# GpSimd is left out of the Fourier stage, its rows lie in four tiles, and the first weights are converted beside the folds

## The chip, the cores and the metric

One core of a Trainium2 chip runs the whole program. The metric is the device time of one execution in microseconds (us); the kernel before takes 2784.65 us, median of three runs from 2784.36 to 2785.43 us. TensorE multiplies matrices, VectorE and ScalarE and GpSimd work on elements, SyncE issues most of the transfers. In the profile they are PE (and PEld for its weight loads), DVE, ACT, POOL and SP.

## What is computed

The reference, cut to what matters:

```python
X = np.fft.fft(np.fft.fft(x, axis=1), axis=2).real         # x: 4 x 3072 x 256
h = X.reshape(-1, 256) @ w_in                              # 256 x 2048
g = np.where(h > 0, h, np.exp(np.minimum(h, 0)) - 1)
y = (g @ w_out).reshape(4, 3072, 256)                      # 2048 x 256
h2 = np.maximum(y @ w_in2, 0)                              # 256 x 1024
u, v = h2[..., :512], h2[..., 512:]
v = (v - mean(v)) / sqrt(var(v) + 1e-6)                    # over the last axis
v = einsum("ts,bsd->btd", w_spatial, v) + b_spatial        # 3072 x 3072
out = (u * v) @ w_out2                                     # 512 x 256
```

The weights arrive as 64-bit numbers, as pairs of 32-bit words, and are converted on the chip.

## The kernel before

The program has four parts on one core: the Fourier transform along the sequence, the first weights (merged with the transform along the 256), the two-layer network, and the product with the 3072 x 3072 matrix. Products are done in three matmuls of a high and a low part (lines 181 to 183), so every operand needs a high part, rounded by ScalarE, and a low part, the rest, by another engine (`split`, lines 145 to 148).

The Fourier stage runs over four batches `b` and three blocks `i` of 128 rows: twelve blocks. For a block the rows and their mirror images (1032 KB, `load_q`) are folded in place into sums and differences (`fold`, seven instructions, lines 253 to 262); four slices of the result are split (`lhs`); TensorE then multiplies them with tables of cosines and sines in eight groups, 36 matmuls (`group`). The sums of a batch are added up in PSUM over its three blocks and copied out by ScalarE in the next batch's first block (`evac`, line 325), two pairs ahead of that block's `lhs` and two behind. In the first batch the tables are split too, a third per block (`split_table`). A single row, number 384, is folded by itself (`rows384`), and three pieces of it are put into row 0 (`row0`).

The order on every engine is the order in which the program is written. Queues run each by themselves and wait only for semaphores, so a transfer on SyncE's queue starts when all the ones ahead of it have been issued and its own buffer is free. In the kernel before a batch's rows lie in one tile of three blocks, two such tiles in turn. GpSimd does the rows 384, most of the tables' low parts, and in the batches after the first parts of the folds of blocks 1 and 2 (lines 253 and 255).

The first weights, 256 x 2048, are converted in eight pieces `q`. `from_f64` (lines 150 to 167) does a piece: two passes of ScalarE (156, 157), VectorE's lines 158, 159, 160 and 165, a multiplication on GpSimd (166) and an addition (167), which is handed back to be done later. VectorE's line 160 is the last that reads the piece as loaded. Pieces 0 to 5 are converted behind the last block, while TensorE does that and the sums of the middle rows (`sum_rows`, tiles `pm`). Pieces 6 and 7 come in the part behind, where the first weights are multiplied with the second transform (tiles `pw`); in the same loop the conversion of twelve pieces of the next weights begins (`late_load`, `late_convert`, `late_split`), two in this loop and one in each of the first ten steps of the network. In these steps the low part of the network's activations (line 607) is shared between VectorE and GpSimd.

Of the kernel before, what the change touches and what calls it, by code (L numbers as in the profile page):

```python
# [123 lines left out]
def fourier_ffn_gated_kernel(ctx: ExitStack, tc: tile.TileContext, t, out: bass.AP):  # L124
# [61 lines left out]
    with ExitStack() as ph:  # L186
# [4 lines left out]
        xop = pool("xop", bufs=4)  # L191
        qp = pool("qp", bufs=2)
        rp = pool("rp", bufs=2)
# [4 lines left out]
        to = [[tp.tile([P, 2, 2 * ODD], F32R, name=f"to{x}{i}") for x in "hl"] for i in range(3)]  # L198
        alt_raw = qp.tile([1, EVE], F32, tag="q", name="alt_raw")
        alt = tp.tile([1, EVE], F32R, name="alt")  # L200
# [7 lines left out]

        def load_q(b, sl):
            if b not in qs:  # L210
                qs[b] = qp.tile([P, 3, 4, 4, ND], F32, tag="q", name=f"q{b}")
            nc.sync.dma_start(qs[b][:, sl], t["xq"][b, :, sl])

# [16 lines left out]
        def split_table(i):  # L230
            v, g = nc.vector, nc.gpsimd
            for k, dst, eng in (("te", te, g if i else v), ("to", to, v if i == 2 else g)):
                for z, raw in enumerate(raw_tables.pop((k, i))):
                    split(dst[i][0][:, z], dst[i][1][:, z], raw, eng)
# [11 lines left out]
        def fold(b, sl, first=None):  # L246


            q, v = qs[b], nc.vector
            w = q[:, sl].rearrange("p i s k d -> p (i s) (k d)")  # L250
            u0, u1, cc, ss = (w[:, :, z * ND : (z + 1) * ND] for z in range(4))
            first = first or v
# [6 lines left out]
            g = q[:, sl].rearrange("p i s k d -> p i (s k) d")  # L259
            near, far = g[:, :, 0:6:5], g[:, :, 8:14:5]  # L260
            v.tensor_tensor(g[:, :, 2:8:5], near, far, op=ALU.add)
            v.tensor_tensor(g[:, :, 10:16:5], near, far, op=ALU.subtract)

        def halves_of(b, sl=slice(0, 3)):
            return qs[b][:, sl].rearrange("p i (h s) k d -> p (i h) (s k d)", h=2)

        def row0(b):

            q, r = halves_of(b), rs[b]
# [4 lines left out]
        def lhs(b, sl):  # L274

            q = halves_of(b, sl)
            ih = slice(2 * sl.start, 2 * sl.stop)
            for k, dst, c0, s0 in (("e", les, 2 * ND, 7 * ND + 1), ("o", los, 4 * ND, ND + 1)):
                if b not in dst:
                    dst[b] = [lp.tile([P, 6, 2, P], F32R, tag=f"l{x}", name=f"l{k}{x}{b}") for x in "hl"]  # L280
                for z, w0 in enumerate((c0, s0)):
                    split(*(x[:, ih, z] for x in dst[b]), q[:, :, w0 : w0 + P])

        def lhs_rest(b):
            q, r = halves_of(b), rs[b]
            for z, slot in ((0, 2), (1, 4)):
                nc.scalar.copy(raw_mids[:, z, :, b : b + 1], q[:, :, slot * ND + P : slot * ND + ND])
# [39 lines left out]

        everything = slice(0, 3)
        load_rows384(0)
        rows384(0)  # L330
        nc.scalar.dma_start(alt_raw, t["alt"])
        for i in range(3):
            load_q(0, slice(i, i + 1))
            if i < 2:
                load_table(i)
            if i == 0:
                load_rows384(1)
        nc.scalar.copy(alt, alt_raw)
        for b in range(B):
            if b:  # L340
                for i in range(3):
                    load_q(b, slice(i, i + 1))
                if b > 1:
                    load_rows384(b)
                rows384(b)
            for i in range(3):
                sl = slice(i, i + 1)
                fold(b, sl, nc.gpsimd if b and i else None)
                if b == 0:
# [6 lines left out]
                if i == 0:  # L356
                    row0(b)
                lhs(b, sl)
# [9 lines left out]
        def in_q(name, dtype):  # L368
            return qp.tile([P, 3, 4, 4, ND], dtype, tag="q", name=name).rearrange("p i s k d -> p (i s k d)")

        st = in_q("conv", U32)
        bits = [st[:, 1024 * x : 1024 * x + 1024].rearrange("p (n w) -> p n w", w=2) for x in range(3)]
        temps = [[st[:, n : n + 512] for n in range(3072 + 1536 * x, 4608 + 1536 * x, 512)] for x in range(2)]

        for q in range(3):
            load_w1(q, bits[q])
        raw_dt = rp.tile([P, 2, 2 * P + 2], F32, tag="r384", name="raw_dt")
# [3 lines left out]
        mid384 = [mp.tile([1, B], F32R, name=f"mid384{x}") for x in "hl"]  # L381
        mid_rows = in_q("mid_rows", F32)[:B, : 4 * EVE].rearrange("b (c n) -> b c n", c=4)
        st3 = lp.tile([P, 1536], U32, tag="lh", name="conv3")
        temps.append([st3[:, n : n + 512] for n in range(0, 1536, 512)])
        row_sums = {}
# [6 lines left out]

        left = None
        for q in range(6):
            mag, num, rest = temps[q % 3]
            left = convert_w1(q, bits[q % 3], mag, num, rest.bitcast(F32), between=left)
            if q + 3 < 6:
                load_w1(q + 3, bits[q % 3])
            if q == 1:
                split(*mids, raw_mids)  # L400
                split(*mid384, raw_mid384)
                evac(B - 1, 0)
            if q == 2:
                split(*dt, raw_dt)
                evac(B - 1, 1)
                for c in range(4):
                    sum_rows(c)
            if q == 3:
                evac(B - 1, 2)
                evac(B - 1, 3)  # L410
        left()
        for c in range(4):
# [75 lines left out]
    with tc.tile_pool(name="w1p", bufs=1, reuse_waits="tile", side="right") as w1p:  # L488
        w1_bits = [wr.tile([P, 512, 2], U32, tag="bits", bufs=2, name=f"w1b{q}") for q in (6, 7)]
        for q in (6, 7):  # L490
            load_w1(q, w1_bits[q - 6])
        QW = 512
# [12 lines left out]
        for q in range(DFF1 // QW):  # L505
# [17 lines left out]
            late_split()  # L523
            if q < 2:
                mag, num, rest = f64_temps(wr, 512)
                convert_w1(6 + q, w1_bits[q], mag, num, rest)()
                late_load(q)
            else:
                late_convert(q - 2)
            for z in range(2):  # L530
# [227 lines left out]
    for s in range(NG + LAG):  # L758
# [10 lines left out]
        late_split()  # L769
        late_convert(s + 2)  # L770
        if step == 0:
# [418 lines left out]
```

## Time and profile before

| | |
|---|---|
| median of three runs | 2784.65 us |
| the profiled execution, by itself | 2789.48 us |
| its span, first to last instruction | 2787.7 us |
| PE busy / DVE / ACT / POOL in the span | 2679.0 / 2107.6 / 1311.1 / 711.2 us |
| last matmul of the Fourier stage's middle rows (`pm`) starts | 138.59 us |
| the steps of the network that convert weights | 177 to 277 us |

A busy share is an average over the whole span. The Fourier stage is only its first twentieth, so what bounds it is read from that stretch alone. A row of a timeline has the start, the duration, the engine, the line, the operation, what is written and read, and in brackets how long the engine was idle before and what ended that. An instruction's duration holds its start-up, so two that follow each other overlap a little.

### The profile page before, as it was taken

What the parts mean: (1) busy time and instruction counts of PE and PEld (TensorE: products, weight loads), DVE (VectorE), ACT (ScalarE), POOL (GpSimd) and SP (SyncE); (2) the same over time, 40 slices, a digit from 0 to 9 for tenths busy, and PEclk for the clock granted to TensorE, in tenths of its full rate; (3) what the DMA queues carried; (4) which work ended last, traced back from release to release, by engine and by line L of the source; (5) the groups of instructions that cost most, each with busy time, mean ns of one, the idle gap of its engine ahead of it and who ended that gap; (6) DMA issues with size and microseconds to landing.
All of it is one profiled execution on the core that took longest, in us unless ns stands there. A gap on an engine that the chain in (4) does not pass through costs nothing.

```text
span 2787.7 us, 35149 instructions
## 1 busy us (share of the span) xinstructions
PE 2679.0 (96%) x12854; PEld 2363.4 (85%) x12854; DVE 2107.6 (76%) x2541; ACT 1311.1 (47%) x1676; POOL 711.2 (26%) x1079
## 2 busy tenths in 40 slices
PE   5867999999999999998999999999999999999999
PEld 5757999999999999997778888888888888888877
DVE  8878888888888888885667767676966577676775
ACT  3456767767767677774322332323233223322332
POOL 5267344455562444555130010000000000000000
PEclk8989999999999999999999999999999999999999
DMA  5531456667675566668799687677866777677683
GB/s 228 171 85 42 145 145 145 152 140 151 138 129 178 138 152 144 145 136 199 248 293 323 235 282 258 238 281 251 293 220 214 269 248 259 232 265 276 224 297 108
DMA packets 212592, 562.72 MB, mean 202 GB/s; under 512 B 24873, under 2 KB 49466, under 8 KB 210882
## 3 DMA queue, kind: packets, MB, share of 16 engines
q1 hardware_dynamic: 146584, 436.68, 44.8%
q0 software_dynamic: 43520, 92.29, 18.2%
q10 hardware_dynamic: 22314, 31.51, 3.1%
q8 instruction: 100, 1.64, 0.2%
q14 instruction: 74, 0.61, 0.1%
HBM read 396.77 MB, written 171.48 MB: 204 GB/s over the span
## 4 chain that ended last, share of the span: by engine, by line
PE 79%; DVE 9%; ACT 5%; DMA 3%; POOL 3%; issue 1%; ACTq 0%; SPq 0%; DVEq 0%; POOLq 0%
PE a L182 17%; PE a L183 16%; PE a L181 16%; PE acc L182 5%; PE acc L183 5%; PE acc L181 5%; DVE glo L607 2%; PE pv L183 1%; DMA u<-uu 1%; PE pv L181 1%; PE pv L182 1%; PE pe L181 1%; ACT ghi L600 1%; PE po L181 1%; PE po L182 1%
## 5 line engine op out<-in xcount | busy, mean ns | idle before, releaser
L182 PE MATMUL a<-wlo,vhi 128*128 128x512 f32 x1920 | 749.4, 390 | 4.5 <-DVE wlo L876 4.5
L183 PE MATMUL a<-whi,vlo 128*128 128x512 f32 x1920 | 749.3, 390 | 1.0 <-DVE vlo L876 1.0
L181 PE MATMUL a<-whi,vhi 128*128 128x512 f32 x1920 | 748.8, 390 | 1.0 <-ACT whi L870 1.0
L870 ACT CAST whi<-raw 128x1024 fp32r<-128x1024 f32 x240 | 252.7, 1053 | 812.6 <-PE a L183 437.0
L876 DVE TENSOR_TENSOR wlo<-raw,whi 128x1024 fp32r<-128x1024 f32 x240 | 293.6, 1223 | 370.2 <-ACT whi L870 369.9
L182 PEld LDWEIGHTS a<-wlo,vhi 128*128 128x128 f32 x1920 | 361.3, 188 | 81.5 <-DVE wlo L876 6.0
L181 PEld LDWEIGHTS a<-whi,vhi 128*128 128x128 f32 x1920 | 361.3, 188 | 77.1 <-ACT whi L870 1.4
L183 PEld LDWEIGHTS a<-whi,vlo 128*128 128x128 f32 x1920 | 361.4, 188 | 76.8 <-DVE vlo L876 1.5
L182 PE MATMUL acc<-glo,wo1h 128*128 128x384 f32 (+1 forms) x1024 | 352.2, 344 | 21.4 <-POOL glo L607 14.8
L183 PE MATMUL acc<-ghi,wo1l 128*128 128x384 f32 (+1 forms) x1024 | 349.6, 341 | 0.0
L181 PE MATMUL acc<-ghi,wo1h 128*128 128x384 f32 (+1 forms) x1024 | 349.5, 341 | 0.0
L607 DVE TENSOR_TENSOR glo<-h,ghi 128x1536 fp32r<-128x1536 f32 (+3 forms) x128 | 231.2, 1806 | 139.3 <-ACT ghi L600 139.3
L915 POOL DMA_DIRECT2D u<-u x32 | 24.4, 763 | 1173.0 <-DVE sum L932 723.2
L860 DVE TENSOR_TENSOR raw<-raw 128x1024 f32<-128x1024 f32 x240 | 293.0, 1221 | 11.0 <-DMA raw<-in_wT 7.8
L593 DVE SCALAR_TENSOR_TENSOR h<-e,h 128x1536 f32<-128x1536 f32 (+1 forms) x128 | 231.9, 1811 | 0.0
L582 ACT ACTIVATE e<-h 128x1536 f32<-128x1536 f32 (+1 forms) x128 | 190.0, 1485 | 88.8 <-DVE h L574 82.2
L182 PEld LDWEIGHTS acc<-glo,wo1h 128*128 128x128 f32 x1024 | 195.8, 191 | 28.4 <-POOL glo L607 17.3
L739 POOL DMA_DIRECT2D v<-v x226 | 204.7, 1259 | 52.9 <-DVE v L693 38.4
L600 ACT CAST ghi<-h 128x1536 fp32r<-128x1536 f32 (+1 forms) x128 | 187.8, 1468 | 24.5 <-DVE h L593 23.9
L183 PEld LDWEIGHTS acc<-ghi,wo1l 128*128 128x128 f32 x1024 | 196.1, 192 | 0.0
L181 PEld LDWEIGHTS acc<-ghi,wo1h 128*128 128x128 f32 x1024 | 195.3, 191 | 0.1
L587 ACT ACTIVATE e<-e 128x1536 f32<-128x1536 f32 (+1 forms) x128 | 190.2, 1486 | 0.0
(202 smaller groups left out, 4463.7 us busy)
## 6 DMA issues: line engine op xcount, KB each, us to landing
raw<-in_wT SPq DMA_DIRECT2D x480, 512.0 KB, 5.5
vlo<-v SPq DMA_DIRECT2D x120, 512.0 KB, 6.0
v<-v POOLq DMA_DIRECT2D x226, 256.0 KB, 5.9
v<-v SPq DMA_DIRECT2D x224, 256.0 KB, 3.0
u<-uu ACTq DMA_DIRECT2D x128, 192.0 KB, 3.3
u<-u POOLq DMA_DIRECT2D x16, 1024.0 KB, 9.4
q<-in_xq SPq DMA_DIRECT2D x12, 1032.0 KB
out<-sum SPq DMA_DIRECT2D x48, 256.0 KB, 2.3
```

The lines of the kernel that those rows point to most:

```text
L181: nc.tensor.matmul(acc, lhsT=w[0], rhs=x[0], start=start, stop=False, skip_group_check=more)
L182: nc.tensor.matmul(acc, lhsT=w[0], rhs=x[1], start=False, stop=False, skip_group_check=more)
L183: nc.tensor.matmul(acc, lhsT=w[1], rhs=x[0], start=False, stop=stop, skip_group_check=more)
L582: nc.scalar.activation(e[:, :, :w], st[s]["h"][:, :, :w], AF.Relu, scale=-1.0)
L587: nc.scalar.activation(e[:, :, :w], e[:, :, :w], AF.Exp, scale=-1.0)
L593: nc.vector.scalar_tensor_tensor(out=h[:, :, :w], in0=e[:, :, :w], scalar=-1.0, in1=h[:, :, :w], op0=ALU.add, op1=ALU.max)
L600: nc.scalar.copy(st[s]["hi"][:, :, :w], st[s]["h"][:, :, :w])
L607: eng.tensor_tensor(st[s]["lo"][:, z, :w], st[s]["h"][:, z, :w], st[s]["hi"][:, z, :w].bitcast(F32), op=ALU.subtract)
L739: nc.gpsimd.dma_start(dst, v, accum_op=ALU.add)
L860: nc.vector.tensor_tensor(res, total, y, op=ALU.add if sg > 0 else ALU.subtract)
L870: nc.scalar.copy(hi, total)
L876: nc.vector.tensor_tensor(lo, total, hi.bitcast(F32), op=ALU.subtract)
```

## The change

Four things are changed. A block's rows get a tile of their own, four in turn (`qp`, `load_q`), and the load of a block's rows is written at the head of that block. What GpSimd did in the Fourier stage goes to VectorE: the row 384, the tables' low parts, its part of the folds; only the multiplication of line 166 stays on GpSimd. The eight pieces of the first weights are converted beside the folds, one per block from the sixth block (batch 1, block 2) on and the eighth behind the last block; each conversion is followed by the load of the piece after the next. Pieces of the next weights take the places of pieces 6 and 7, so that the conversion ends two steps earlier in the network.

```diff
-        qp = pool("qp", bufs=2)
+        qp = pool("qp", bufs=4)
+        cvp = pool("cvp", bufs=1)
...
-        def load_q(b, sl):
-            if b not in qs:
-                qs[b] = qp.tile([P, 3, 4, 4, ND], F32, tag="q", name=f"q{b}")
-            nc.sync.dma_start(qs[b][:, sl], t["xq"][b, :, sl])
+        def load_q(b, i):
+            q = qs[b, i] = qp.tile([P, 4, 4, ND], F32, tag="q", name=f"q{b}{i}")
+            nc.sync.dma_start(q, t["xq"][b, :, i])
...
-            v, g = nc.vector, nc.gpsimd
-            for k, dst, eng in (("te", te, g if i else v), ("to", to, v if i == 2 else g)):
+            for k, dst in (("te", te), ("to", to)):
...
-            r, g = rs[b], nc.gpsimd
+            r, g = rs[b], nc.vector
...
-            first.tensor_tensor(w[:, :, : 2 * ND], w[:, :, : 2 * ND], w[:, :, 2 * ND :], op=ALU.add)
+            v.tensor_tensor(w[:, :, : 2 * ND], w[:, :, : 2 * ND], w[:, :, 2 * ND :], op=ALU.add)
             v.tensor_tensor(cc, u0, u1, op=ALU.add)
-            (v if b < 2 else first).tensor_tensor(ss, u0, u1, op=ALU.subtract)
+            v.tensor_tensor(ss, u0, u1, op=ALU.subtract)
...
+        def load_bits(q):
+            if q < 8:
+                raw = bits_at[q] = cvp.tile([P, 512, 2], U32, tag="bits", bufs=2, name=f"w1b{q}")
+                load_w1(q, raw)
+
+        def convert(q):
+            if left:
+                left.pop()()
+            if q < 8:
+                left.append(convert_w1(q, bits_at.pop(q), *f64_temps(cvp, 512)))
+                load_bits(q + 2)
...
         for b in range(B):
-            if b:
-                for i in range(3):
-                    load_q(b, slice(i, i + 1))
-                if b > 1:
-                    load_rows384(b)
-                rows384(b)
             for i in range(3):
-                sl = slice(i, i + 1)
-                fold(b, sl, nc.gpsimd if b and i else None)
+                if b:
+                    load_q(b, i)
+                if b == 1 and i == 1:
+                    load_bits(0)
+                    load_bits(1)
+                if b and i == 0:
+                    if b > 1:
+                        load_rows384(b)
+                    rows384(b)
+                fold(b, i)
...
                 if i == 2:
                     lhs_rest(b)
+                if b > 1 or b == 1 and i == 2:
+                    convert(step)
+                    step += 1
                 for c in range(4):
                     for z in range(2):
                         group(b, c, z, [i])
...
-        parts = [(nc.vector, slice(0, 2))] if s > len(late) - 2 else [(nc.vector, slice(0, 1)), (nc.gpsimd, slice(1, 2))]
+        parts = [(nc.vector, slice(0, 2))] if s > len(late) - 4 else [(nc.vector, slice(0, 1)), (nc.gpsimd, slice(1, 2))]
...
-        late_convert(s + 2)
+        late_convert(s + 4)
```

On SyncE's queue of the kernel before, from the last rows of batch 1 to the weights (`q1` to `q3` are the batches' tiles, `r384` the row 384, `conv` the tile of weights pieces):

```order
L212 DMA q1_493<-in_xq 128x2064 [waits DMAHW2_49]
L212 DMA q2_695<-in_xq 128x2064 [waits DMAHW3_49,DMAHW5_49,DVE_49,Activation_49]
L212 DMA q2_695<-in_xq 128x2064 [waits DMAHW7_49]
L212 DMA q2_695<-in_xq 128x2064 [waits DMAHW1_49]
L207 DMA r384_2_699<-in_x384 1x1032 [waits DMAHW2_49,DVE_49]
L212 DMA q3_899<-in_xq 128x2064 [waits DMAHW0_49,DVE_49,DMAHW3_49,Activation_49,Pool_49]
L212 DMA q3_899<-in_xq 128x2064 [waits DMAHW5_49]
L212 DMA q3_899<-in_xq 128x2064 [waits DMAHW7_49]
L207 DMA r384_3_903<-in_x384 1x1032 [waits DMAHW1_49,DVE_49]
L170 DMA conv_1103<-in_moe_w_in 128x1024 [waits DVE_49,DMAHW3_49,Activation_49,Pool_49]
```

Three loads of rows stand together, the weights behind all of them. The same queue now, from the last rows of batch 1 on (`q12` is batch 1, block 2; `w1b2` the weights piece 2):

```order
L212 DMA q12_652<-in_xq 128x2064 [waits DMAHW4_49,DVE_49,Activation_49]
L170 DMA w1b2_686<-in_moe_w_in 128x1024 [waits DMAHW2_49,DVE_49,Activation_49]
L212 DMA q20_726<-in_xq 128x2064 [waits DMAHW3_49]
L208 DMA r384_2_728<-in_x384 1x1032 [waits DMAHW5_49]
L170 DMA w1b3_786<-in_moe_w_in 128x1024 [waits DMAHW0_49,DVE_49,Activation_49]
L212 DMA q21_832<-in_xq 128x2064 [waits DMAHW1_49]
L170 DMA w1b4_862<-in_moe_w_in 128x1024 [waits DMAHW2_49,DVE_49,Activation_49]
L212 DMA q22_900<-in_xq 128x2064 [waits DMAHW3_49]
```

From batch 2 on a load of weights, which waits for VectorE and ScalarE, stands ahead of each load of rows. VectorE's queue now, from the low parts of batch 2, block 1, to the fold of block 2 (lines 251 to 260 are the fold's, `cv` the conversion's tiles):

```order
L148 TENSOR_TENSOR lol2_760<-q21_832,loh2_759 128x2x128 [waits Activation_49] x2
L167 TENSOR_TENSOR raw_w1l_219<-cv2_778,cv1_777 128x512 [waits Pool_49]
L158 TENSOR_SCALAR cv0_852<-cv0_852 128x512 [waits Activation_49]
L159 TENSOR_SCALAR cv1_853<-cv0_852 128x512 [waits DVE_49]
L160 SCALAR_TENSOR_TENSOR cv1_853<-w1b2_686,cv1_853 128x512 [waits DMAHW2_49,DVE_49]
L165 TENSOR_SCALAR cv0_852<-cv1_853 128x512 [waits DVE_49]
L251 TENSOR_TENSOR q22_900<-q22_900 128x4x258 [waits DMAHW3_49]
L252 TENSOR_TENSOR q22_900<-q22_900 128x4x129 [waits DVE_49]
L253 TENSOR_TENSOR q22_900<-q22_900 128x4x129
```

The five instructions of a conversion now stand between the low parts of a block and the next fold, and the fold's first instruction is back on VectorE.

## Rows read from the trace of the kernel before

**Rows 1.** Stretches: start:end length, busy us (instructions) of PE, PEld, DVE, ACT, POOL.

```profile
0.00:47.50 47.50, 20.43 (x76) 18.36 (x76) 40.64 (x38) 16.18 (x33) 30.05 (x24) 0.86 0.58 233
...
277.00:287.00 10.00, 10.00 (x59) 10.00 (x58) 8.65 (x14) 7.63 (x7) 5.00 (x8) 1.00 0.41 150
```

**Rows 2.** Waits to 128.8 us: total us, times, longest.

```profile
ACT leh L147 <- DVE q L262: 52.8, 8, 12.5
...
PE pa L181 <- ACT leh L147: 33.8, 5, 14.7
```

**Rows 3.** Timeline of VectorE: start, us, line, written<-read [idle before].

```profile
14.10 1.82 DVE L148 TENSOR_TENSOR tel<-raw_te,teh 128x770 fp32r<-128x770 f32 x2
...
47.63 1.22 DVE L253 TENSOR_TENSOR q<-q 128x1032 f32<-128x1032 f32 x1
48.88 0.69 DVE L254 TENSOR_TENSOR q<-q 128x516 f32<-128x516 f32 x1
...
51.90 0.42 DVE L262 TENSOR_TENSOR q<-q 128x258 f32<-128x258 f32 x1
53.97 0.76 DVE L148 TENSOR_TENSOR lel<-q,leh 128x256 fp32r<-128x256 f32 x2 [1.65 <-issue]
54.65 0.75 DVE L148 TENSOR_TENSOR lol<-q,loh 128x256 fp32r<-128x256 f32 x2
...
62.39 3.90 DVE L254 TENSOR_TENSOR q<-q 128x516 f32<-128x516 f32 x1
...
111.39 0.76 DVE L148 TENSOR_TENSOR lel<-q,leh 128x256 fp32r<-128x256 f32 x2 [0.47 <-ACT leh L147]
```

**Rows 4.** Timeline of VectorE, conversion of pieces 0 and 1 of the weights.

```profile
118.10 0.43 DVE L158 TENSOR_SCALAR conv<-conv 128x512 f32<-128x512 f32 x1 [0.28 <-ACT conv L156]
...
119.03 0.69 DVE L160 SCALAR_TENSOR_TENSOR conv<-conv 128x512 uint32<-128x512 uint32 x1
119.75 0.43 DVE L165 TENSOR_SCALAR conv<-conv 128x512 uint32<-128x512 uint32 x1
...
120.55 1.40 DVE L159 TENSOR_SCALAR conv<-conv 128x512 uint32<-128x512 uint32 x1
...
122.59 0.68 DVE L167 TENSOR_TENSOR raw_w1h<-conv 128x512 f32<-128x512 f32 x1
```

**Rows 5.** Timeline of GpSimd: a fold's first sum, and the conversion's multiplication.

```profile
63.72 2.01 POOL L253 TENSOR_TENSOR q<-q 128x1032 f32<-128x1032 f32 x1
...
120.32 1.34 POOL L166 TENSOR_TENSOR conv<-conv 128x512 f32<-128x512 f32 x1 [22.32 <-DVE conv L165]
```

**Rows 6.** Timeline: issue of the first rows, and VectorE's first instruction.

```profile
1.14 0.36 SPq L212 DMA_DIRECT2D q<-in_xq  x1
...
6.08 1.48 DVE L253 TENSOR_TENSOR q<-q 128x1032 f32<-128x1032 f32 x1 [6.08 <-DMA q<-in_xq]
```

**Rows 7.** Transfers to 185 us: queue, times, KB each, median us to landing.

```profile
a<-xo ACTq DMA_DIRECT2D x12, 384.0 KB, 7.8
conv<-in_moe_w_in SPq DMA_DIRECT2D x6, 512.0 KB, 4.2
```

**Rows 8.** Timeline of ScalarE: last store of an evacuation; a conversion's first pass.

```profile
57.03 0.52 ACTq L326 DMA_DIRECT2D a<-xo  x1
...
117.41 0.66 ACT L156 ACTIVATE conv<-conv 128x512 f32<-128x512 f32 x1
```

**Rows 9.** Stretches at two clocks (the last three: PE's clock, DMA share, GB/s).

```profile
102.00:106.00 4.00, 4.00 (x14) 4.00 (x13) 3.01 (x6) 1.81 (x5) 0.00 (x0) 0.50 1.01 361
107.00:111.00 4.00, 4.00 (x24) 4.00 (x24) 3.78 (x9) 2.32 (x7) 0.00 (x0) 1.00 0.83 313
```

**Rows 10.** Timeline of TensorE: first and last of 56 matmuls of the middle rows.

```profile
128.83 0.34 PE L181 MATMUL pm<-teh,midsh 128*4 128x386 f32 x1
...
138.59 0.34 PE L183 MATMUL pm<-toh,midsl 128*4 128x384 f32 x1
```

**Rows 11.** Timeline of VectorE: the same instruction in two steps of the network.

```profile
259.58 0.55 DVE L573 TENSOR_TENSOR h<-q,po 128x384 f32<-128x384 f32 x1 [1.18 <-POOL glo L607]
...
269.44 0.55 DVE L573 TENSOR_TENSOR h<-q,po 128x384 f32<-128x384 f32 x1 [1.18 <-POOL glo L607]
```

More of the change, by code (lines that the diff above doesn't have):

```diff
@@ L198, in fourier_ffn_gated_kernel @@
         to = [[tp.tile([P, 2, 2 * ODD], F32R, name=f"to{x}{i}") for x in "hl"] for i in range(3)]
-        alt_raw = qp.tile([1, EVE], F32, tag="q", name="alt_raw")
+        alt_raw = cvp.tile([1, EVE], F32, tag="cv0", name="alt_raw")
         alt = tp.tile([1, EVE], F32R, name="alt")
@@ L244, in rows384, with fold @@
             g.tensor_tensor(rv[:, 1, : 2 * ND], rv[:, 0, 2 * ND :], rv[:, 1, 2 * ND :], op=ALU.subtract)
-        def fold(b, sl, first=None):
-            q, v = qs[b], nc.vector
-            w = q[:, sl].rearrange("p i s k d -> p (i s) (k d)")
+        def fold(b, i):
+            q, v = qs[b, i], nc.vector
+            w = q.rearrange("p s k d -> p s (k d)")
             u0, u1, cc, ss = (w[:, :, z * ND : (z + 1) * ND] for z in range(4))
-            first = first or v
-            first.tensor_tensor(w[:, :, : 2 * ND], w[:, :, : 2 * ND], w[:, :, 2 * ND :], op=ALU.add)
+            v.tensor_tensor(w[:, :, : 2 * ND], w[:, :, : 2 * ND], w[:, :, 2 * ND :], op=ALU.add)
             v.tensor_tensor(cc, u0, u1, op=ALU.add)
-            (v if b < 2 else first).tensor_tensor(ss, u0, u1, op=ALU.subtract)
+            v.tensor_tensor(ss, u0, u1, op=ALU.subtract)
             x, y = w[:, 0::2], w[:, 1::2]
@@ L258, in fold, with halves_of @@
             v.tensor_tensor(y[:, :, : 2 * ND], x[:, :, 2 * ND :], y[:, :, 2 * ND :], op=ALU.subtract)
[L259 to L265, printed above, removed]
+            g = q.rearrange("p s k d -> p (s k) d")
+            near, far = g[:, 0:6:5], g[:, 8:14:5]
+            v.tensor_tensor(g[:, 2:8:5], near, far, op=ALU.add)
+            v.tensor_tensor(g[:, 10:16:5], near, far, op=ALU.subtract)
+        def halves_of(b, i):
+            return qs[b, i].rearrange("p (h s) k d -> p h (s k d)", h=2)
         def row0(b):
-            q, r = halves_of(b), rs[b]
+            q, r = halves_of(b, 0), rs[b]
             nc.scalar.copy(q[0:1, 0, 7 * ND : 8 * ND], r[:, 1, 1])
@@ L272, in row0, with lhs @@
             nc.scalar.copy(q[0:1, 1, 4 * ND : 5 * ND], r[:, 1, 0])
-        def lhs(b, sl):
-            q = halves_of(b, sl)
-            ih = slice(2 * sl.start, 2 * sl.stop)
+        def lhs(b, i):
+            q = halves_of(b, i)
+            ih = slice(2 * i, 2 * i + 2)
             for k, dst, c0, s0 in (("e", les, 2 * ND, 7 * ND + 1), ("o", los, 4 * ND, ND + 1)):
@@ L282, in lhs @@
                     split(*(x[:, ih, z] for x in dst[b]), q[:, :, w0 : w0 + P])
+            for z, slot in ((0, 2), (1, 4)):
+                nc.scalar.copy(raw_mids[:, z, ih, b : b + 1], q[:, :, slot * ND + P : slot * ND + ND])
         def lhs_rest(b):
-            q, r = halves_of(b), rs[b]
-            for z, slot in ((0, 2), (1, 4)):
-                nc.scalar.copy(raw_mids[:, z, :, b : b + 1], q[:, :, slot * ND + P : slot * ND + ND])
+            r = rs[b]
             nc.scalar.copy(raw_mid384[:, b : b + 1], r[:, 0, 0, P:])
@@ L326, in evac @@
             nc.scalar.dma_start(a_d[b][c], xo[:, :, :n])
-        everything = slice(0, 3)
+        bits_at, left = {}, []
+        def load_bits(q):
[8 more added lines that the diff above has]
+                load_bits(q + 2)
         load_rows384(0)
@@ L332, in fourier_ffn_gated_kernel @@
         for i in range(3):
-            load_q(0, slice(i, i + 1))
+            load_q(0, i)
             if i < 2:
@@ L338, in fourier_ffn_gated_kernel @@
         nc.scalar.copy(alt, alt_raw)
+        step = 0
         for b in range(B):
-            if b:
-                for i in range(3):
-                    load_q(b, slice(i, i + 1))
-                if b > 1:
-                    load_rows384(b)
-                rows384(b)
-            for i in range(3):
-                sl = slice(i, i + 1)
-                fold(b, sl, nc.gpsimd if b and i else None)
+            for i in range(3):
+                if b:
[8 more added lines that the diff above has]
+                fold(b, i)
                 if b == 0:
@@ L357, in fourier_ffn_gated_kernel @@
                     row0(b)
-                lhs(b, sl)
+                lhs(b, i)
                 if b and i == 0:
@@ L366, in fourier_ffn_gated_kernel @@
                         group(b, c, z, [i])
[L368 to L376, printed above, removed]
         raw_dt = rp.tile([P, 2, 2 * P + 2], F32, tag="r384", name="raw_dt")
@@ L381, in fourier_ffn_gated_kernel @@
         mid384 = [mp.tile([1, B], F32R, name=f"mid384{x}") for x in "hl"]
-        mid_rows = in_q("mid_rows", F32)[:B, : 4 * EVE].rearrange("b (c n) -> b c n", c=4)
-        st3 = lp.tile([P, 1536], U32, tag="lh", name="conv3")
-        temps.append([st3[:, n : n + 512] for n in range(0, 1536, 512)])
+        mid_rows = qp.tile([P, 4, EVE], F32, tag="q", name="mid_rows")[:B]
         row_sums = {}
@@ L391, in sum_rows @@
                 sum_block(acc[:B], c, 0, rows, rows, i, mid384 if c == 0 else None)
[L393 to L411, printed above, removed]
+        split(*mids, raw_mids)
+        split(*mid384, raw_mid384)
+        convert(step)
+        assert step == 7
+        split(*dt, raw_dt)
+        evac(B - 1, 0)
+        evac(B - 1, 1)
+        for c in range(4):
+            sum_rows(c)
+        evac(B - 1, 2)
+        evac(B - 1, 3)
+        convert(8)
         for c in range(4):
@@ L488, in fourier_ffn_gated_kernel @@
     with tc.tile_pool(name="w1p", bufs=1, reuse_waits="tile", side="right") as w1p:
-        w1_bits = [wr.tile([P, 512, 2], U32, tag="bits", bufs=2, name=f"w1b{q}") for q in (6, 7)]
-        for q in (6, 7):
-            load_w1(q, w1_bits[q - 6])
+        late_load(0)
+        late_load(1)
         QW = 512
@@ L523, in fourier_ffn_gated_kernel @@
             late_split()
[L524 to L529, printed above, removed]
+            late_convert(q)
             for z in range(2):
```

2 lines of the change are left out of this document (1 added, 1 removed).

## The prediction

> **What bounds the kernel now.** I read the stages first (busy time by stretch), then the waits, then VectorE's own timeline. After 277 us the matrix engine is without a gap (10.00 busy of 10.00 [rows 1]), so whatever this change does, it does before 277 us. In the Fourier stage TensorE is busy 20.4 of the first 47.5 us, VectorE 40.6 [rows 1]; the waits say why: TensorE waited 33.8 us for ScalarE's casts, and these 52.8 us for the last instruction of VectorE's fold [rows 2]. So VectorE sets the pace of the Fourier stage. In the stretch from 177 to 277 us another chain does: each step waits for GpSimd, 9.86 us from step to step (259.58 to 269.44 [rows 11]).
>
> The stage is a row of twelve blocks (four batches by three). Of a block VectorE does a fold of seven instructions and four low parts, "lhs". In the timeline a fold that nobody disturbs runs from 47.63 to 52.32 us, 4.7 us [rows 3]; then VectorE waits for ScalarE, 1.65 us where row 0 has to be patched first, 0.47 us elsewhere, and the four low parts take 1.4 us [rows 3]. The same instruction that takes 0.69 us there took 3.90 us at 62.39 us, when GpSimd was folding too [rows 3, 5]. That is what the change removes.
>
> **The change, part by part.** I follow VectorE through the stage of the new kernel, in us from the span's start.
>
> Blocks 0 to 2. The first fold starts as before when its rows land, at 6.1 [rows 6]. To it come all the tables' low parts, four of 0.87 each (1.82 for two, less the overlap [rows 3]), 3.5 per block: 4.7 + 3.5 + 1.4 = 9.6. The casts that these wait for are done in the cover of the fold. Three blocks and the small row (0.2) end at 6.1 + 29.0 = 35.1, where the fourth block began at 47.63 before [rows 3]: 12 us gained.
>
> Blocks 3 to 5. The five operations on the row 384 come to VectorE, ahead of the batch's first fold. No row shows them there; by the fold's instructions of as many elements (0.69 for 516, 0.42 for 258 [rows 3], the ends overlapped) they take about 2.1, between 1.4 (five short ones) and 3.5 (five long ones). Block 3: 2.1 + 4.7 + 1.65 + 1.4 = 9.9, to 45.0. Block 4: 4.7 + 0.5 + 1.4 = 6.6, to 51.6. Block 5 the same and 0.2, to 58.4. Then the first piece of the weights: 0.3 of waiting and 1.6 from L158 to the end of L160 (118.10 to 119.72 [rows 4]), to 60.3.
>
> Blocks 6 to 11. Here I part from what the words of the change suggest. On SyncE's queue the load of the next rows now stands behind the load of weights piece q+2, and that one waits until piece q was read for the last time, by VectorE's L160. L160 is followed on VectorE by one instruction, L165 (0.43 [rows 4], 0.35 of it before the next), and then by the next fold, which needs those rows. So six times (blocks 6 to 11) the fold waits a whole load: issue of the weights' load, issue of the rows' load, landing. Queued behind the waiting load are only the rows, and in blocks 6 and 9 row 384. The landing: the first rows, with nothing ahead, were there 4.9 us after their issue [rows 6], half a megabyte of weights after 4.2 [rows 7]. The two together move 1.5 MB; at the 361 GB/s that a busy stretch shows [rows 9] the second half-megabyte costs 1.4 more, so 4.9 + 1.4 = 6.3, less what overlaps with the first one's start-up: I take 6.0, and 6.2 where row 384 is last. From below it is 4.9, from above 7.8 (the stores' landing beside other loads [rows 7]). Before, the rows of whole batches were queued together and landed long ahead, so nothing of this shows there.
>
> A block of the usual kind, from L160 to L160: 6.0 landing + 4.7 fold + 0.5 + 1.4 lhs + 0.6 for L167 (0.68 [rows 4], overlapped) + 1.6 = 14.8. There are four: 59.2, and 0.4 for two small rows. The first of a batch: 6.2 + 2.1 + 4.7 + 1.65 + 1.4, then VectorE waits until ScalarE has evacuated two more pairs (done 2.2 after the last low part [rows 3, 8]) and done the first pass over the piece (0.66 [rows 8]): 2.8; then 1.6. Sum 20.45, twice: 40.9. In the batch's first two blocks four stores of 384 KB go out beside the loads: 0.77 MB a block, some 1.5 us each in four blocks, 6.0, between 0 and 12. Together 106.5: the last L160 ends at 60.3 + 106.5 = 166.8.
>
> GpSimd's eight multiplications stay (1.34 [rows 5]). They run right after L165, while VectorE waits for rows, and I cost them at nothing. The Trainium skill (SBUF — State Buffer, "SBUF: two separate sides") speaks against that if the cover goes: VectorE and GpSimd share one pair of ports under an exclusive lock, and the loser is blocked until the other's instruction is over. By that rule each multiplication beside a fold would hold VectorE up by up to its 1.3 us; this trace has 1.40 against 0.43, 0.97 lost beside such a multiplication [rows 4, 5].
>
> The tail. The last block's casts begin 4.0 before that L160, at 162.8. TensorE then has 38 matmuls. After a wait it goes at half clock, 14 in 4 us at 0.50 against 24 at 1.00 [rows 9]; 38 take 6.3 at the upper level and 10.9 at the lower. It has just waited: I take 9.0, to 171.8. The 56 matmuls of the middle rows took 10.1 (128.83 to 138.93 [rows 10]) and still follow: 181.9 against 138.9, so **43.0 later**. What converts pieces 6 and 7 after 139.7 us is replaced by pieces of the next weights with the same chain, no difference.
>
> Given back: two steps of the stretch to 277 us no longer carry a conversion. A step of 36 matmuls is 6.1 us where TensorE is full (59 in 10 us [rows 1]); VectorE's part is close, so I take 6.4 against 9.86 [rows 11]: 2 x 3.5 = **7.0 earlier**, between 4 and 7.5. What is late next there is TensorE itself.
>
> Sum: +43.0 - 7.0 = **+36**. The profiled execution took 2789.5 us (span 2787.7), 4.8 above the median of the runs, 2784.65; I carry the difference to the median: **2821 us**, 1.3% slower.
>
> **The rivals.** (1) *The loads come early after all.* If the rows were there when the fold begins, as they were in every block before, the six landings and the stores' 6.0 go (36.4 + 6.0), and L165's 0.35 counts six times: the last L160 at 126.5, TensorE, which is full then, done at 139.1, +0.2 - 7.0, 2778; with the multiplications now beside folds, 6 x 0.97, 2784. I put it at 2781. For it: VectorE has 12 us in hand by block 3. Against it: the queue's order, which no spare time changes. It decides from the point where a stall is under about 1 us. By the skill's lock all of the 1.3 would be lost each time, and it would end at 2786. (2) *TensorE sets the pace* and hides the stalls: at half clock throughout, 440 matmuls take 126 us from 14 on, with the middle rows 150, +11 - 7, 2789. For it: the half clock after each wait [rows 9]. Against it: 36 matmuls at the lower level are 10.3 us, a stalled block 14.8. (3) *The landings are as slow as the stores were*, 7.8 each [rows 7], and the stores cost double: +10.8 + 6.0, 2838. For it: loads and stores do meet in blocks 6, 7, 9 and 10; against it: the queue holds two loads at a time now, not three or four.
>
> **How the numbers follow.** Forecast 0.82, rival 1 0.08, rival 2 0.03, rival 3 0.07. The likeliest case alone: landing -6.6 to +10.8, stores -6 to +6, row 384 -2 to +4, last block -2.7 to +1.9, steps -0.5 to +3; not all on one side, so 2804 to 2838. The range is **2800 to 2841**: it takes rival 3 in and leaves out 1 and 2 and a little of the ends. A difference under 0.2%, 5.6 us, can't be told from none. Rival 1 lies on that edge: half of it is faster; its other half, rival 2 and a rest are "same". Faster 0.04, same 0.07, slower 0.89.
>
> **What would show it.** Right: VectorE idle some 5 to 6 us six times before the fold's first instruction (L251), put down to the rows' DMA; SyncE waiting for VectorE's L160 ahead of each weights' load; no folding instruction over 1.5 us; the fourth fold near 37 us; the middle rows' last matmul near 182; two fewer steps of 9.9 us. Wrong: rows landed before L160 ends, blocks 6 to 11 under 10 us each, or TensorE and not VectorE the one that is waited for there. The forecast falls if the middle rows end before 146 us.

## The result, and the profile after

The changed kernel took **2824.15 us** (median of 4 runs, 2822.35 to 2826.48), the kernel before 2785.04 us beside it (4 runs, 2784.36 to 2788.06): ratio 1.0137, interval 1.0121 to 1.0153. It is 39 us slower, where the prediction said 36 (2821). The profiled execution has a span of 2821.6 us, against 2787.7 before: 33.9 more.

The stretches of the kernel after, with the columns of [rows 1] (the last three are TensorE's clock, DMA share and GB/s):

```profile
0.00:34.70 34.70, 18.03 (x76) 15.95 (x76) 30.38 (x51) 16.56 (x37) 0.19 (x4) 0.99 0.87 350
34.70:59.00 24.30, 24.26 (x121) 23.26 (x121) 21.87 (x43) 10.97 (x35) 0.00 (x0) 0.88 0.18 66
59.00:162.00 103.00, 51.23 (x218) 47.56 (x218) 56.03 (x108) 24.50 (x74) 7.73 (x6) 0.71 0.35 126
...
167.70:178.00 10.30, 10.15 (x58) 4.50 (x55) 0.69 (x1) 3.40 (x9) 0.80 (x2) 1.00 0.60 198
178.00:214.00 36.00, 22.17 (x73) 13.75 (x74) 19.69 (x26) 17.67 (x33) 23.57 (x19) 0.87 0.34 97
```

The first half of the Fourier stage is faster now: three blocks in 34.7 us (47.5 before), the next three in 24.3 with TensorE full. The other half, 59 to 162 us, has nobody busy: TensorE 51 of 103 us, VectorE 56, DMA 0.35. Where every engine is half idle, look for a chain in which each waits for the next. The waits up to 200 us (total us, times, longest) show it: TensorE waits for ScalarE, ScalarE for VectorE's fold, VectorE for the rows. SyncE's queue, asked by itself, gives the reason:

```profile
PE pa L181 <- ACT leh L147: 63.5, 7, 11.9
ACT leh L147 <- DVE q L260: 62.3, 8, 12.0
DVE q L251 <- DMA q<-in_xq: 24.5, 5, 5.7
DVE r L239 <- DMA r<-in_x: 16.5, 3, 7.3
```

```profile
SPq L170 <- DVE cv L160: 116.1, 6, 33.4
```

VectorE waits for rows whose load SyncE has not issued yet, because SyncE itself stands at the weights' load until VectorE is through L160. One turn of this in SyncE's timeline, and then in VectorE's (start, us, line; in brackets the idle time before and who ended it):

```profile
95.09 0.33 SPq L170 DMA_DIRECT2D w1b<-in_moe_w_in  x1
95.46 0.43 SPq L212 DMA_DIRECT2D q<-in_xq  x1
```

```profile
34.73 0.68 DVE L239 TENSOR_TENSOR r<-r 1x516 f32<-1x516 f32 x1
...
36.91 1.22 DVE L251 TENSOR_TENSOR q<-q 128x1032 f32<-128x1032 f32 x1
...
58.29 0.69 DVE L160 SCALAR_TENSOR_TENSOR cv<-w1b,cv 128x512 uint32<-128x512 uint32 x1
...
66.37 0.69 DVE L239 TENSOR_TENSOR r<-r 1x516 f32<-1x516 f32 x1 [6.92 <-DMA r<-in_x]
...
94.33 0.69 DVE L160 SCALAR_TENSOR_TENSOR cv<-w1b,cv 128x512 uint32<-128x512 uint32 x1
95.06 0.43 DVE L165 TENSOR_SCALAR cv<-cv 128x512 uint32<-128x512 uint32 x1
101.24 1.23 DVE L251 TENSOR_TENSOR q<-q 128x1032 f32<-128x1032 f32 x1 [5.75 <-DMA q<-in_xq]
102.50 0.70 DVE L252 TENSOR_TENSOR q<-q 128x516 f32<-128x516 f32 x1
...
109.53 0.69 DVE L160 SCALAR_TENSOR_TENSOR cv<-w1b,cv 128x512 uint32<-128x512 uint32 x1
...
118.03 0.68 DVE L239 TENSOR_TENSOR r<-r 1x516 f32<-1x516 f32 x1 [7.34 <-DMA r<-in_x]
...
161.28 0.69 DVE L160 SCALAR_TENSOR_TENSOR cv<-w1b,cv 128x512 uint32<-128x512 uint32 x1
...
214.27 0.56 DVE L567 TENSOR_TENSOR h<-q,po 128x386 f32<-128x386 f32 x1
...
292.07 0.56 DVE L567 TENSOR_TENSOR h<-q,po 128x384 f32<-128x384 f32 x1 [1.18 <-POOL glo L601]
...
298.10 0.55 DVE L567 TENSOR_TENSOR h<-q,po 128x384 f32<-128x384 f32 x1
...
304.01 0.56 DVE L567 TENSOR_TENSOR h<-q,po 128x384 f32<-128x384 f32 x1
```

L160 ends at 95.02; SyncE issues the weights at 95.09 and the rows at 95.46; VectorE begins the fold at 101.24. Six such waits, 5.60 to 7.34, make 37.05 us.

Two more readings, from TensorE's and GpSimd's timelines. The middle rows start 38.9 us later than in [rows 10] (167.75 against 128.83) and take as long:

```profile
167.75 0.34 PE L181 MATMUL pm<-teh,midsh 128*4 128x386 f32 x1
...
177.52 0.34 PE L183 MATMUL pm<-toh,midsl 128*4 128x384 f32 x1
```

And GpSimd's list in one round of the weights stage's loop, which follows (the first line is one of the eight multiplications in the Fourier stage):

```profile
95.66 1.29 POOL L166 TENSOR_TENSOR cv<-cv,cv 128x512 f32<-128x512 f32 x1 [13.50 <-DVE cv L165]
...
189.50 1.30 POOL L166 TENSOR_TENSOR cv<-cv,cv 128x512 f32<-128x512 f32 x1 [1.61 <-DVE cv L165]
190.87 1.26 POOL L167 TENSOR_TENSOR cv<-cv,cv 128x512 f32<-128x512 f32 x1
192.09 1.27 POOL L148 TENSOR_TENSOR w1l<-raw_w1h,w1h 128x512 fp32r<-128x512 f32 x1
193.33 1.29 POOL L148 TENSOR_TENSOR w1l<-raw_w1l,w1h 128x512 fp32r<-128x512 f32 x1
194.58 1.46 POOL L148 TENSOR_TENSOR wo1l<-cv,wo1h 128x512 fp32r<-128x512 f32 x1
197.65 1.30 POOL L166 TENSOR_TENSOR cv<-cv,cv 128x512 f32<-128x512 f32 x1 [1.62 <-DVE cv L165]
```

It is busy for 6.6 of the 8.15 us of a round. In the kernel before, the first two rounds converted pieces whose addition was on VectorE and that had no low part `wo1l`; its first combine of the network, which ends the loop's work, stood here (VectorE's timeline of before):

```profile
171.93 0.56 DVE L573 TENSOR_TENSOR h<-q,po 128x386 f32<-128x386 f32 x1
```

171.93 there and 214.27 after (L567): 42.3 later, 3.4 more than the middle rows. Lines 292.07, 298.10 and 304.01 above are the network's steps that were 9.86 in [rows 11]: two of them now take 6.03 and 5.91, and give 7.8 back. From there to the end the distance stays between 31 and 36 us.

### The profile page after: what moved, and what is told of

Read it like the earlier page. It is cut to its first block, busy times and chain, and to the rows that moved or that the text cites. A ratio compares the mean times of both kernels' runs of the same rounds, so it can differ in the third digit from the quotient of the medians.

```text
span 2821.6 us, 35140 instructions
## 1 busy us (share of the span) xinstructions
PE 2680.0 (95%) x12854; PEld 2366.2 (84%) x12854; DVE 2095.1 (74%) x2579; ACT 1313.3 (47%) x1692; POOL 655.0 (23%) x1039
## 4 chain that ended last, share of the span: by engine, by line
PE 80%; DVE 9%; ACT 4%; DMA 4%; POOL 2%; issue 1%; ACTq 0%; SPq 0%; DVEq 0%; POOLq 0%
PE a L182 16%; PE a L183 16%; PE a L181 16%; PE acc L182 5%; PE acc L183 5%; PE acc L181 5%; DVE glo L601 1%; PE pv L181 1%; PE pv L182 1%; PE pv L183 1%; PE pe L181 1%; PE po L181 1%; PE po L182 1%; PE po L183 1%; PE pe L182 1%; PE pe L183 1%
## 5 line engine op out<-in xcount | busy, mean ns | idle before, releaser
L601 DVE TENSOR_TENSOR glo<-h,ghi 128x1536 fp32r<-128x1536 f32 (+2 forms) x128 | 234.3, 1830 | 139.1 <-ACT ghi L594 138.7
L594 ACT CAST ghi<-h 128x1536 fp32r<-128x1536 f32 (+1 forms) x128 | 187.9, 1468 | 25.2 <-DVE h L587 23.8
```

The lines of the kernel that those rows point to most:

```text
L594: nc.scalar.copy(st[s]["hi"][:, :, :w], st[s]["h"][:, :, :w])
L601: eng.tensor_tensor(st[s]["lo"][:, z, :w], st[s]["h"][:, z, :w], st[s]["hi"][:, z, :w].bitcast(F32), op=ALU.subtract)
```

## The experiments

The kernel before was run beside them again: 2787.4, 2787.6 and 2787.1 us (medians of 15 runs each), so ratios, and not single microseconds, are compared between groups. All kernels compute the whole reference.

**Is it the place of the rows' load?** e1 issues the rows of block n+1 at the head of block n, ahead of the piece's conversion; e2 does so from the last batch on only (blocks 9 to 11). The conversion, the folds and every other instruction stay.

```diff
-                if b:
-                    load_q(b, i)
+                n = 3 * b + i
+                if 3 <= n < 4:            # e2: < 9
+                    load_q(b, i)
+                if 4 <= n + 1 < 12:       # e2: 9 <=
+                    load_q(*divmod(n + 1, 3))
+                    if n % 3 == 2:
+                        load_rows384(b + 1)
...
-                    if b > 1:
+                    if 1 < b and 3 * b < 4:   # e2: < 9
```

> The changed kernel with one thing undone: the load of a block's rows is issued at the head of the block before it, ahead of that block's conversion and so ahead of the weights' load that waits for it. Theory 1 (the rows wait behind the weights' load): the six waits for rows on VectorE, 37 us in the trace of the changed kernel, go to under 1 us each; blocks 6 to 11 take 9 to 10 us instead of 15; with up to 1 us a block lost to the multiplications that now fall beside folds, about 2785 us, between 2778 and 2793. Rival 2 (what VectorE took over from GpSimd, and the conversions, are the price; the landings only lie in time it would need anyway): 2810 us or more. Rival 3 (TensorE falls to half clock in the long blocks and stays the slower one): the waits go, but the time stays above 2800 us.

> As e1, but only batch 3's rows are loaded a block ahead; batch 2's three blocks still wait. Theory 1: three of the six waits remain (18 us in the trace of the changed kernel), so the time lies half way between the changed kernel and e1, about 2805 us, 2799 to 2811. Rivals 2 and 3: no more than a quarter of the way, above 2815 us.

Measured: e1 2794.21 us, ratio 1.0022 (1.0013 to 1.0031), 1 us above the expected range; e2 2809.0, 1.0074 (1.0059 to 1.0089). The middle rows' last matmul, at 177.52 in the change, is now here (e1, then e2):

```profile
145.59 0.34 PE L183 MATMUL pm<-toh,midsl 128*4 128x384 f32 x1
```

```profile
162.29 0.34 PE L183 MATMUL pm<-toh,midsl 128*4 128x384 f32 x1
```

So the early load takes away 32 of the 39 us (by the ratios, and by the middle rows), and half of the stalls half of it: the place on the queue is the cause. What is left over in e1 teaches as much: it is still 7 us late at the middle rows, and a block takes 10.1 to 10.3 us from L160 to L160, the first of a batch 15.2 to 15.3, where 9 to 10 were expected. VectorE's and GpSimd's timelines of e1, where the multiplication now runs beside the fold:

```profile
74.53 1.23 DVE L251 TENSOR_TENSOR q<-q 128x1032 f32<-128x1032 f32 x1
75.79 1.67 DVE L252 TENSOR_TENSOR q<-q 128x516 f32<-128x516 f32 x1
```

```profile
74.78 2.12 POOL L166 TENSOR_TENSOR cv<-cv,cv 128x512 f32<-128x512 f32 x1 [13.69 <-DVE cv L165]
```

L252 takes 1.67 instead of 0.70 and L166 2.12 instead of 1.29: with the stall gone, the cover that I had named for the multiplications is gone too, and 0.97 is lost, the number of [rows 4] (1.40 against 0.43). The Trainium skill's exclusive lock (SBUF — State Buffer, "SBUF: two separate sides"), under which the second to come waits until the other's instruction is over, fits both numbers: L166 begins 0.98 before L251 ends and takes 0.83 longer, and L252 begins 1.11 before L166 ends and takes 0.97 longer. Each pays about what is left of the other's running instruction, and not the whole of it.

**The same, by the queue alone.** e9 leaves the rows' loads where the change put them and issues weights pieces 2 to 7 on GpSimd's queue.

```diff
-        nc.sync.dma_start(bits, t["moe_w_in"]...)
+        (nc.gpsimd if q > 1 else nc.sync).dma_start(bits, t["moe_w_in"]...)
```

> The changed kernel, with the loads of weights pieces 2 to 7 issued on GpSimd's queue instead of SyncE's; not one instruction of VectorE, ScalarE or TensorE is moved, and the loads of rows stay where they stand. Theory (the six stalls come from the place on SyncE's queue alone: the rows' load stands behind a load that waits for VectorE's L160): the stalls go, and the time is that of e1, 2794 (2788 to 2799; a little more where GpSimd's issuing costs, a little less where rows come several blocks ahead). Rival (the rows' load is late because tiles come free late or because the transfers are slow): the stalls stay, 2815 to 2825.

Measured: 2790.65 us (11 runs, 2785.56 to 2794.86), ratio 1.0011 (1.0002 to 1.002). GpSimd's timeline and SyncE's waits:

```profile
74.75 2.11 POOL L166 TENSOR_TENSOR cv<-cv,cv 128x512 f32<-128x512 f32 x1 [13.01 <-DVE cv L165]
76.81 0.59 POOL L170 DMA_DIRECT2D w1b<-in_moe_w_in  x1
```

```profile
SPq L212 <- DVE lol L148: 60.4, 8, 12.4
```

SyncE now waits only for a tile of rows to come free, and after the first block no fold waits for rows. This changes no instruction but the engine that issues six loads: rows that stood behind a load waiting for L160 were the whole stall.

**GpSimd in the folds, or not.** e3 is e1 with the two parts of the fold on GpSimd that the kernel before has there.

```diff
+            first = nc.gpsimd if b and i else v
-            v.tensor_tensor(w[:, :, : 2 * ND], ...
+            first.tensor_tensor(w[:, :, : 2 * ND], ...
-            v.tensor_tensor(ss, u0, u1, op=ALU.subtract)
+            (v if b < 2 else first).tensor_tensor(ss, u0, u1, op=ALU.subtract)
```

> e1 with GpSimd's part of the folds as in the kernel before (line 253 of blocks 1 and 2 of batches 1 to 3, line 255 of batches 2 and 3). Theory 1a (GpSimd beside VectorE costs more than it takes off): VectorE's instructions beside it go from 0.7 to 2 us and more, 5 to 12 us slower than e1. Rival (GpSimd's 1.8 us per block is a gain, the slow-down is small): 5 to 10 us faster than e1.

Measured: 2801.55 us, ratio 1.0047 (1.003 to 1.0064), 7.3 more than e1, and the middle rows end 9.1 later. With the conversion beside the folds, leaving GpSimd out of the folds is a gain by itself.

**Conversion behind the last block.** e4 is the changed kernel with no conversion in the blocks; the eight pieces follow them.

```diff
-                if b > 1 or b == 1 and i == 2:
-                    convert(step)
-                    step += 1
...
-        convert(step)
-        assert step == 7
+        convert(0)
+        convert(1)
...
-        convert(8)
+        for q in range(4, 9):
+            convert(q)
```

> The changed kernel with the first weights converted behind the last block instead of beside the folds; rows, tiles and engines as changed. No load of rows is then queued behind a weights' load. Theory 1: no wait for rows at all, the folds end near 103 us, the conversions (some 4 us each on VectorE and GpSimd) near 137 us, and the whole takes about 2780 us, 2774 to 2790. Rival 2 (VectorE's taken-over folds and tables are the price): still above 2805 us.

Measured: 2779.41 us, ratio 0.9972 (0.9961 to 0.9984): faster than the kernel before, and by the ratios 46 us faster than the change. From block 5's last low part to block 11's, e4 needs 44.5 us, e1 71.0 with six pieces between: 4.4 a piece. VectorE's timelines of the two, e4 first:

```profile
56.86 0.28 DVE L148 TENSOR_TENSOR e384l<-r,e384h 1x128 fp32r<-1x128 f32 x1
...
101.38 0.28 DVE L148 TENSOR_TENSOR e384l<-r,e384h 1x128 fp32r<-1x128 f32 x1
```

```profile
56.71 0.28 DVE L148 TENSOR_TENSOR e384l<-r,e384h 1x128 fp32r<-1x128 f32 x1
...
127.73 0.28 DVE L148 TENSOR_TENSOR e384l<-r,e384h 1x128 fp32r<-1x128 f32 x1
```

Behind the last block a piece takes some 4.27. So laying the conversion beside the folds hides nothing even without stalls: a piece is 2.67 us on VectorE (0.43 + 0.43 + 0.69 + 0.43 + 0.69), and VectorE is the engine that sets the pace there (in e1 busy 61.0 of 71 us, with waits for ScalarE alone). The rest of the 4.4 is the 0.97 beside the multiplication and, in the first block of a batch, 2.6 of waiting for ScalarE's first pass over the piece. In e4 the rest of a piece is a wait, the line of VectorE's timeline and, from the last block on, the sum:

```profile
105.72 0.69 DVE L167 TENSOR_TENSOR raw_w1h<-cv,cv 128x512 f32<-128x512 f32 x1 [1.47 <-POOL cv L166]
```

```profile
ACT cv L156 <- POOL cv L166: 16.3, 7, 3.0
```

**Does GpSimd's list hold the weights stage's loop?** e5 puts the additions L167 of its four rounds on VectorE.

```diff
-            from_f64(raw, ..., mag, num, rest, nc.gpsimd)()
+            from_f64(raw, ..., mag, num, rest, nc.gpsimd if n > 3 else None)()
```

> The changed kernel, with the additions of the first four late pieces (L167 in the weights stage's loop) on VectorE instead of GpSimd; nothing else. Theory (the loop, 7.4, 8.2 and 8.2 us per round in the changed kernel, is a chain through GpSimd: multiplication, addition, two low parts of w1, low part of the late piece): each of four rounds loses the addition's 1.3 us from that chain, against some 0.7 on VectorE that lies beside GpSimd's low parts; about 4 to 5 us of the 2825 go (2817 to 2822), and the combine that follows the loop stands that much nearer to the end of pm. Rival (the round is held by ScalarE's casts or by TensorE, and GpSimd's list only fills it): no change, 2824 to 2827.

Measured: 2821.9 us, ratio 1.0123 (1.0109 to 1.0137), which overlaps the change's 1.0121 to 1.0153: undecided by time. In the trace ScalarE's L156 of the first and the fourth round are 21.9 us apart (186.29 to 208.21) instead of 23.8 (185.25 to 209.01): 1.8 gained of the 3.8 that three additions would make. The addition is part of the chain, not all of it; what holds the rest stays open. In the profiled execution of e5 the middle rows come 1.8 us later than in the change's, ahead of anything that the edit touches, and that takes the gain back.

**A multiplication on VectorE.** e8 is e1 with L166 of the first weights on VectorE.

```diff
...
-        nc.gpsimd.tensor_tensor(rest, rest, magf, op=ALU.mult)
+        (nc.vector if early else nc.gpsimd).tensor_tensor(rest, rest, magf, op=ALU.mult)
```

> e1 (rows loaded a block ahead) with the eight multiplications L166 on VectorE instead of GpSimd. Theory (beside VectorE's folds each multiplication on GpSimd costs VectorE 0.98 us, as e1's trace shows at L252 and L240): VectorE's own multiplication takes about 0.69, so each block gets some 0.3 us shorter and the waits for the hand-over go; e1's 2794.2 becomes 2791 (2786 to 2794). Rival (what VectorE seems to lose there lies in waits that it has anyway): 8 times 0.69 are added, 2798 to 2801.

Measured: 2789.07 us (11 runs, 2787.58 to 2793.13), ratio 1.0009 (1.0 to 1.0018). The time lies in the expected range, but not for the reason given. The block gets only 0.17 shorter (L160 to L160 9.91 instead of 10.08), the last one in the blocks begins 0.8 earlier (128.61, in e1 129.44), and the middle rows' last matmul starts at 145.67, in e1 at 145.59: there TensorE ends the stage, and its granted clock from 126 to 136 us was 0.67 in e8, 0.83 in e1. At 1030 us the two profiled executions are 1.8 us apart, by 1297 us 5.1, and there the edit has nothing. e1, e8 and e9, whose middle rows end within 1.6 us of each other, measured 2794, 2789 and 2791: a difference of 5 us between runs of different groups is not to be explained by an edit.

**How far it goes.** e6 gives e4's pieces a second set of temporaries, e7 adds e5's edit, e10 the multiplications on VectorE and a third buffer for the loads, e11 one of two low parts of w1 on VectorE.

```diff
+                if q % 2:                                              # e6
+                    st = qp.tile([P, 3, 512], U32, tag="q", name=f"cq{q}")
+                    temps = [st[:, 0], st[:, 1], st[:, 2].bitcast(F32)]
...
-                ...tag="bits", bufs=2, name=f"w1b{q}")
+                ...tag="bits", bufs=3, name=f"w1b{q}")                 # e10
...
-                split(wh[:, kt], wl[:, kt], ..., nc.gpsimd)
+                split(wh[:, kt], wl[:, kt], ..., None if kt else nc.gpsimd)   # e11
```

> e4 (conversions behind the last block), with a second set of the three temporaries, so that a piece's steps on ScalarE and VectorE needn't wait until GpSimd has multiplied the piece before; the addition of a piece follows the third VectorE step of the next. Theory (e4's 4.27 us per piece is 2.67 of VectorE's own five steps and 1.5 of waiting for GpSimd's multiplication): about 2.8 per piece, so some 10 us less than e4's 2779.4: 2769 (2766 to 2773). Rival (the pieces' loads, two buffers of 0.5 MB at some 4.2 us a landing, set the pace): as e4, 2777 to 2781.

> e6 and e5's edit together. If both gains are on the path that sets the end, e6's time less some 5 us: about 2764 (2760 to 2769). If the loop isn't held by GpSimd: e6's time.

> e7 with the first weights' multiplications on VectorE, and a third buffer for their loads. In e6's trace a piece took 3.6 us instead of the 2.8 expected: one VectorE step in each was 1.40 instead of 0.43, beside GpSimd's multiplication, and ScalarE waited 1.5 to 2.5 us for the pieces' loads in six of eight. Theory (both are costs): a piece takes VectorE's own 3.36 at most, eight of them 2 us less than now: 2771 (2768 to 2774), e7 having 2773.4. Rival (VectorE's 0.69 takes the place of what it lost, and nothing is gained): 2773 to 2776.

> e10, with one of the two low parts of w1 of each round of the weights stage's loop on VectorE (0.69) instead of GpSimd (1.3). Theory (with the additions gone from GpSimd its list is still in the chain of two rounds of four): 1 to 2 us less than e10. Rival (the loop is now the chain ScalarE's cast, VectorE's steps, multiplication, addition, and GpSimd's low parts fill its waits): as e10.

Measured: e6 2775.59 (ratio 0.9956, 0.9944 to 0.9969); e7 2773.41 (0.9951, 0.9938 to 0.9963); e10 2769.24 (0.9933, 0.992 to 0.9945); e11 2767.04 (0.9929, 0.9916 to 0.9943). e6 missed: 4 us gained instead of 10. VectorE's and ScalarE's timelines of e6 show both of the costs that I had left out:

```profile
104.55 1.40 DVE L159 TENSOR_SCALAR cq<-cq 128x512 uint32<-128x512 uint32 x1
```

```profile
115.55 0.67 ACT L156 ACTIVATE cv<-w1b 128x512 f32<-128x512 f32 x1 [1.52 <-DMA w1b<-in_moe_w_in]
```

In nearly every piece one VectorE step lost 0.8 to 1.0 beside GpSimd's multiplication, and ScalarE waited 1.0 to 2.6 us for the loads of six pieces. e10 takes the first away and leaves of the second two waits, of 0.84 and 0.56, which VectorE doesn't feel; its timeline shows a piece in 3.25 us instead of 3.6:

```profile
109.68 0.69 DVE L160 SCALAR_TENSOR_TENSOR cv<-w1b,cv 128x512 uint32<-128x512 uint32 x1
...
112.93 0.69 DVE L160 SCALAR_TENSOR_TENSOR cq<-w1b,cq 128x512 uint32<-128x512 uint32 x1
```

e7 over e6 (2 us, where 5 were expected) and e11 over e10 are within what these runs can tell. The best version is 0.7% faster than the kernel before; it keeps the change's folds and tiles and undoes its conversion beside the folds.

## Why the prediction was right

The mechanism and its place held; the sizes, point by point:

| term | predicted | measured |
|---|---|---|
| blocks 0 to 2 end | 35.1 | 34.7 |
| row 384 on VectorE | 2.1 | 2.2 (34.73 to 36.91) |
| block 5's L160 ends | 60.3 | 59.0 |
| L160's end to the block's first instruction, blocks 6 to 11 | 36.4 in six | 39.9 in six (VectorE idle 37.05) |
| wait where row 0 is patched, blocks 3, 6 and 9 | 1.65 each | 0.73 to 0.74 each |
| a usual block, L160 to L160 | 14.8 | 14.8 to 15.2 |
| first block of a batch | 20.45 | 21.25 and 21.66 |
| stores beside the loads | 6.0 | at most 2.8, see below |
| blocks 6 to 11 in all | 106.5 | 103.0 |
| last L160 to the middle rows | 5.0 | 5.8 |
| the middle rows | +43.0 | +38.9 |
| weights stage's loop | 0 | +3.4 |
| two steps of the network | -7.0 | -7.8 |
| sum, profiled executions | +36 | +33.9 |

*The mis-sized terms.* The largest is the stores' 6.0, set at 1.5 in each of four blocks. In blocks 7 and 10 it is nothing: the second pair of stores goes out before those blocks' loads (in batch 2 at 75.83 and 77.34, the loads from 80.30), and VectorE waits 5.60 and 5.72, no longer than in the blocks without stores. In blocks 6 and 9 two stores do meet the loads, and from L160's end to VectorE's first instruction there it is 7.39 and 7.81 where the sum had 6.2: 2.8 for both. That is the stores and not row 384, whose load stands behind the rows. In the profile's list of transfers the rows issued at 59.43 land after 8.0 us, those issued at 95.46, with no store beside them, after 5.8; row 384 was there first, and its five instructions (66.37 to 68.56) cover what the rows came later. The prediction's price came from stores that landed beside three or four loads in the kernel before [rows 7].

The wait where row 0 is patched was taken from one row of the kernel before, 1.65 [rows 3]; it came out at 0.73 to 0.74 in all three blocks, 2.8 less together. In the kernel before ScalarE patches at 52.87, right behind the issue of an evacuation's store (52.17 to 52.75) and after the fold has ended; in block 3 of the changed kernel that store is out at 39.85, and ScalarE patches at 41.30, as soon as the fold's L259 is done (41.27). Against both stands the loop of the weights stage, which I costed at "no difference" because the chain is the same for each piece. It isn't: the new pieces bring an addition and a low part to GpSimd. GpSimd's list, with the length of each line, was in the trace of before (one round of 1.29 + 1.27 + 1.29 there); it should have been added up. Of the 3.4, e5 gets 1.8 back by moving the additions; the rest was not taken apart.

The measured terms add up to +34.5 (38.9 + 3.4 - 7.8), and the profile has +33.9. That the forecast came so near is in part luck: 4.1 us too many up to the middle rows and 3.4 too few in the loop nearly cancel.

*From the profile to the time.* The sum was made against the profiled execution and carried to the median of the runs. The two profiled executions differ by 33.9, the medians by 39: before's profiled execution was some 4 us above its median, after's 0.8 below. Part of the closeness of 2821 to 2824 is that, and not the sum. Against the later runs of the kernel before, 2787.1 to 2787.6, the change is some 37 us slower.

*The eight multiplications.* Six of them cost nothing, as said, and for the reason given: in the change they run while VectorE waits for rows (1.28 to 1.29 each, and no folding instruction above 1.23 from 60 us on). For the last two, behind the folds, VectorE waited 1.30 and 1.18. e1 is the case in which the cover goes, and there each of the six costs VectorE the 0.97. The prediction's "all of the 1.3" was too much: when VectorE's instruction comes, 1.1 of the multiplication is left.

*The rivals.* (1) did not happen, but e1 and e9 are what it describes, and it was priced at 2781; they took 2794 and 2791, 0.2% and 0.1% above the kernel before. The step that fails in that pricing is "TensorE, which is full then": in e1 TensorE is at clock 0.80 from 59 to 130 us and busy 52.5 of 71, the last L160 ends at 130.1 instead of 126.5, and 5.7 us of matmuls still stand between it and the middle rows. (2) fell: TensorE waits 63.5 us for ScalarE's casts in the first 200 us. (3) fell as a whole, since four of the six waits were 5.60 to 5.75; in block 6 the rows' landing, 8.0, is what it describes.

## What to carry to other kernels

A DMA queue is a list in order: a load that waits for a consumer holds back every load behind it, so look, for each load that you move, at what stands behind it on its queue and who needs that; moving the waiting load to an idle engine's queue cost one line here and took the stalls away. Work that you lay "beside" something is hidden only from engines that don't do it: ask which engine sets the pace there, and whether the moved work runs on that same engine.

## What the runs showed of the hardware

GpSimd and VectorE slow each other, and both lose: the multiplication of 128x512 takes GpSimd 1.29 alone and 2.12 beside VectorE's fold, and one VectorE instruction gets 0.97 longer. In e1 each loses about what was left of the other's running instruction, 0.83 of 0.98 and 0.97 of 1.11.

TensorE pays for a wait after it too. In a stall of the changed kernel and behind it:

```profile
82.00:86.00 4.00, 0.50 (x3) 0.17 (x1) 0.00 (x0) 0.00 (x0) 0.16 (x1) 0.88 0.90 370
86.50:94.00 7.50, 2.51 (x8) 2.51 (x9) 6.89 (x14) 2.56 (x8) 0.00 (x0) 0.50 0.00 0
```

It was busy 0.50 of 4 us while the rows came in, and its granted clock in the stretch that follows is 0.50, the lower of its two levels. Between the blocks of the changed kernel this cost little, since TensorE waited again for VectorE anyway. Behind the last block nothing hides it: from the casts' start (157.73) to the middle rows (167.75) it took 10.0 us, where the prediction had 9.0.
